# Transposing k and q of chunks 10 to 23 on VectorE, from blocked loads, in an attention and MLP kernel

## The chip, the cores and the metric

The kernel runs on one core of one Trainium2 chip. The metric is the device time of one execution in microseconds (us). Each version is run several times, and its median counts. The profile shows one further execution.

## What is computed

A linear attention with decay, followed by a two-layer MLP with a leaky ReLU, all in 32-bit floats:

```python
# q, k, v: (B, H, S, D) = (4, 8, 768, 64); lam: one decay per head; blocks of 64 tokens
for b in range(S // 64):
    qb, kb, vb = (block b of q, k, v)
    intra = einsum('bhic,bhjc->bhij', qb, kb) * Dmask        # lam ** (i - j) where i >= j, else 0
    intra = einsum('bhij,bhjd->bhid', intra, vb)
    inter = einsum('bhid,bhde->bhie', qb * lam_pow, kv_state)
    out[block b] = intra + inter
    kv_state = lam ** 64 * kv_state + einsum('bhsd,bhse->bhde', kb * rev_pow, vb)
x = out, tokens by (heads * D)                               # 3072 x 512
h = x @ w_in                                                 # 512 x 2048
out = maximum(0.01 * h, h) @ w_out                           # 2048 x 512
```

The weights come as 64-bit words, which the kernel converts itself.

## The kernel before, in words

**Chunks and rounds.** The 3072 tokens are cut into 24 chunks of 128 tokens (`NCH`), six to a batch entry. Four chunks make a group of 512 tokens (`GC`, `T`), so there are six groups. Chunks 0 to 3 run alone, chunk 4 is begun early, and from then on `round_of(c)` holds one chunk's attention, in a software pipeline: it loads k and q of chunk c + 2 (`load_kq`), computes chunk c's outputs (`outputs`), and in between chunk c + 1's scores and state update (`scores`). From round 8 on, the transposes of chunk c + 2 follow these on TensorE. Matrix products of the attention are 64x64 products on quadrants of TensorE (`quad`, L286).

**Transposes.** The scores need k and q with the head dimension on the partitions (`kTs`, `qTs`), and the loads bring tokens on the partitions (`kqv`). `transposes(c)` makes four TensorE transposes for k (into the upper part of `po`) and four for q (into `pt`), all on L331. ScalarE copies them to SBUF (L340, L341). Then GpSimd scales k in place by the decay (L345), which the state update reads, and the transposed q into `qsTs` (L349). `kqv`, `kTs`, `qTs` and `qsTs` have two buffers each, for even and odd chunks. VectorE multiplies the scores with the decay mask (L375) and updates the state (L382).

**Projections.** A chunk's result leaves `po` as three parts, `xh`, `xl`, `xm` (L430 on ScalarE, L431 and L433 on VectorE), which carry the 32-bit precision through three passes of the matrix product. `up(g, p)` multiplies a group with one of eight blocks of `w_in` (L561): two blocks of 512 columns, each with a scaling on ScalarE between the passes (L579) and the leaky ReLU into one of two `gs` buffers (L582), after which SP stores the buffer to the scratch tensor `G` (L585). `down` (L620) runs when all `up` steps are done, and reads `G` back.

**Weights.** `to_float32` turns 64-bit words into 32-bit floats: a load into one of three buffers `raw`, three passes on ScalarE (L497, L499, L501) and two on VectorE (L503, L504). The `w_in` blocks are converted in the first 90 us. The `w_out` blocks (`w_out`) are converted during groups 2 and 3, one for every two `up` steps, and stored to a scratch tensor `WO` (L538), from where they are read late.

**What sets the order.** Nothing is issued as it is written. Each operation is given to a planner (`Plan.add`) with its engine, an estimated duration in us, and the names of the buffers it reads and writes. `Plan.emit` simulates the engines with these estimates, always takes the operation that can start first (the smaller rank, the place in the list `seq`, breaks ties), and issues all in that order. Each engine then works strictly through its own order. All DMA loads and stores apart from `w_in`'s are issued on SP's queue, so a load that has to wait there holds up all that is behind it.

Of the kernel before, what the change touches and what calls it, by code (L numbers as in the profile page):

```python
# [31 lines left out]
def _bc(ap, idx, n):  # L32
    a = [list(x) for x in ap.ap]
    return bass.AP(ap.tensor, ap.offset, a[:idx] + [[0, n]] + a[idx:])


class Plan:
# [23 lines left out]
    def add(self, eng, us, fn, reads=(), writes=(), rank=0.0):  # L61

        n, deps = len(self.ops), set()
        for k in reads:
            w, r = self.last.setdefault(k, [None, []])
            if w is not None:
                deps.add(w)
            r.append(n)
        for k in writes:
            w, r = self.last.setdefault(k, [None, []])  # L70
            if w is not None:
                deps.add(w)
            deps.update(r)
            self.last[k] = [n, []]
        deps.discard(n)
        ways = {eng: us} if isinstance(eng, str) else dict(zip(eng, us))
        if self.chain is not None:
            self.chains[self.chain].append(n)
        self.ops.append((ways, fn, deps, (self.rank + rank, n), set(writes)))
# [81 lines left out]
def kernel(  # L161
# [10 lines left out]
    nc = tc.nc  # L172
    P = 128
    B, H, SEQ, D = q.shape
    C, C2 = P, P // 2
    NCB = SEQ // C
    HP = H // 2
    d_model, d_ff = moe_w_in.shape
    KO = d_model // P
    NP = d_ff // (2 * P)  # L180
    NCH = B * NCB
    GC = 4
    NG = NCH // GC
    T = GC * C
# [3 lines left out]
    QS = 0  # L188
    KM = 1
    NRAW = 3  # L190
    HALF = (slice(0, D), slice(D, 2 * D))
    assert D == 64 and KO == HP == 4 and SEQ % C == 0 and NCH % GC == 0 and d_model == T == 512 and NP % 4 == 0

    pool = ctx.enter_context(tc.tile_pool(name="sb", bufs=1))
    psum = ctx.enter_context(tc.tile_pool(name="ps", bufs=1, space=bass.MemoryType.PSUM))
# [3 lines left out]
    def sb(shape, name, dt=F32):  # L199
        return pool.tile(shape, dt, name=name, tag=name)  # L200

    def ps(shape, name):
        return psum.tile(shape, F32, name=name, tag=name)


    pt = ps([P, HP, C], "pt")
# [6 lines left out]
    X = [[sb([P, KO, T], f"x{x}{i}", F32R) for x in "hlm"] for i in range(2)]  # L213
    raw = [sb([P, 2 * d_model], f"raw{i}") for i in range(NRAW)]
    lows = [sb([P, d_model], f"low{i}", I32) for i in range(2)]
# [11 lines left out]
    def part(n):  # L227
        nonlocal used
        used += n
        assert used <= NA, used  # L230
        return att[:, used - n:used]

    ident = part(P)
    kqv = [[part(H * D).rearrange("p (h d) -> p h d", h=H) for _ in range(2)] for _ in range(3)]
    kTs, qTs, qsTs = ([part(HP * C).rearrange("p (y t) -> p y t", y=HP) for _ in range(2)] for _ in range(3))
    sc = part(2 * HP * C2).rearrange("p (x y t) -> p x y t", x=2, y=HP)
    state = [part(HP * D).rearrange("p (y d) -> p y d", y=HP) for _ in range(4)]
# [21 lines left out]
    add = plan.add  # L259
# [10 lines left out]
    def factors_q():  # L270
        for i in range(2):
            nc.vector.tensor_copy(lam_p[HALF[i]], lam_h[HALF[i], i::2])
        for hp in range(HP):
# [11 lines left out]
    def quad(dst, rows, lhsT, rhs, cols, start=False):  # L285
        nc.tensor.matmul(dst[HALF[cols]], lhsT=lhsT[HALF[rows]], rhs=rhs[HALF[rows]], start=start, stop=True,  # L286
                         skip_group_check=True)
# [11 lines left out]
    def of(c):  # L299
        return c // NCB, c % NCB, c % 2  # L300
# [3 lines left out]
    def load_kq(c):  # L304
        b, n, i = of(c)
        for src, x, nm in ((k, 0, "k"), (q, 1, "q")):
            y, dst = src[b, :, n * C:(n + 1) * C, :], kqv[x][i]

            def go(y=y, dst=dst):
                for z in range(2):  # L310
                    nc.sync.dma_start(out=dst[:, z * HP:(z + 1) * HP, :], in_=y[z::2].rearrange("h p d -> p h d"))  # L311
            add("DMA", 1.15, go, [], [f"{nm}{i}"])

    def load_v(c):
        b, n, i = of(c)
# [3 lines left out]
    def transposes(c):  # L319
        b, n, i = of(c)  # L320
        tk, tq = kqv[0][i], kqv[1][i]
        if c < GC:
            z, key = bank[KT].rearrange("p (y t) -> p y t", y=HP), KT
            at = [z[:, y, :] for y in range(HP)]
        else:
            z, key = po[:, :, upper, :], "po"
            at = [po[:, y // 2, HP + y % 2 * 2:HP + y % 2 * 2 + 2, :].rearrange("p a t -> p (a t)") for y in range(HP)]

        def go(src, at):
            for y in range(HP):  # L330
                nc.tensor.transpose(out=at[y], in_=src[:, 2 * y:2 * y + 2, :].rearrange("p a d -> p (a d)"), identity=ident)  # L331

        add("PE", 0.44, lambda: go(tk, at), [f"k{i}"], [key])
        add("PE", 0.44, lambda: go(tq, [pt[:, y, :] for y in range(HP)]), [f"q{i}"], ["pt"])

        def copies():
            kT = kTs[i]
            into = kT if c < GC else kT.rearrange("p (t a) x -> p t (a x)", t=2)
            src = z if c < GC else z.rearrange("p t a x -> p t (a x)")
            add("ACT", 0.6, lambda: nc.scalar.copy(into, src), [key], [f"kT{i}"])  # L340
            add("ACT", 0.6, lambda: nc.scalar.copy(qTs[i], pt), ["pt"], [f"qT{i}"])  # L341
            kr = tk.rearrange("p (y x) d -> p y x d", x=2)
            nr = slice(0, C2 if n == NCB - 1 else P)
            add(*((("DVE", "POOL"), (0.7, 1.1)) if c < KM else ("POOL", 1.1)),
                lambda e="POOL": ENG[e].tensor_tensor(kr[nr], kr[nr], _bc(pow_k, 3, D)[nr], op=ALU.mult), ["fk"], [f"k{i}"])  # L345
            m = slice(1 if n == 0 else 0, 2)
            o, x = (z.rearrange("p y (t i) -> p y t i", t=2)[:, :, m, :] for z in (qsTs[i], pt if c < QS else qTs[i]))
            eng, e, us, dep = ("DVE", nc.vector, 0.7, "pt") if c < QS else ("POOL", nc.gpsimd, 1.2, f"qT{i}")
            add(eng, us, lambda: e.tensor_tensor(o, x, _bc(pow_q, 2, 2)[:, :, m, :], op=ALU.mult), ["fq", dep], [f"qsT{i}"])  # L349

        return copies
# [121 lines left out]
    n_raw = 0  # L473

    def to_float32(kind, p, h, dst, key, after=()):

        nonlocal n_raw
        j, n_raw = n_raw % len(raw), n_raw + 1
        r, low, kl = raw[j], lows[n_raw % 2], f"low{n_raw % 2}"
        d = dst.bitcast(I32)  # L480

        def load():
            r64 = r.bitcast(I64)
            if kind == "wi":
                nc.scalar.dma_start(out=r64.rearrange("p (k f) -> p k f", k=2),
                                  in_=w_in_r[:, 2 * h:2 * h + 2, p * 2 * P:(p + 1) * 2 * P])
            else:
                nc.sync.dma_start(out=r64, in_=moe_w_out[(2 * p + h) * P:(2 * p + h + 1) * P, :])

        def words(i, dt):  # L490
            return r.bitcast(dt).rearrange("p (n two) -> p n two", two=2)[:, :, i]

        def addend(dt, i):
            return low.bitcast(dt).rearrange("p (n two) -> p n two", two=2)[:, :, i]

        add("DMA", 1.6, load, after, [f"raw{j}"])
        add("ACT", 0.67, lambda: nc.scalar.activation(out=dst, in_=words(1, F32), func=AF.Abs, scale=2.0 ** -110),  # L497
            [f"raw{j}"], [key])
        add("ACT", 0.78, lambda: nc.scalar.activation(out=addend(U16, 0), in_=words(0, U32), func=AF.Copy, bias=0.0, scale=2.0 ** -29),  # L499
            [f"raw{j}"], [kl])  # L500
        add("ACT", 0.77, lambda: nc.scalar.activation(out=addend(F16, 1), in_=words(1, F32), func=AF.Copy, bias=0.0, scale=2.0 ** -100),  # L501
            [f"raw{j}"], [kl])
        add("DVE", 0.42, lambda: nc.vector.tensor_scalar(d, d, 3, None, op0=ALU.logical_shift_left), [], [key])  # L503
        add("DVE", 1.0, lambda: nc.vector.tensor_tensor(d, d, low, op=ALU.add), [kl], [key])  # L504
# [159 lines left out]
    nxt, n_out = 3 * GC, 0  # L664
    steps = [(g, p) for g in range(2, NG) for p in range(NP)]
    for n, (g, p) in enumerate(steps):
        while nxt < (g + 1) * GC:
            seq.append(("r", nxt))
            nxt += 1
        seq.append(("up", g, p))  # L670
        if nxt < NCH and nxt // GC < g + 2 and n % 2 == 0:
            seq.append(("r", nxt))
            nxt += 1
        if n_out < NP and n % 2 == 1:
            seq.append(("wo", n_out, ["G%d%d" % steps[n - 1]]))
            n_out += 1
        if g == NG - 1:
            seq.append(("wp", p))
# [5 lines left out]
    for n, x in enumerate(seq):  # L684
# [9 lines left out]
        elif x[0] == "wp":  # L694
            if not freed:
                add("DVE", 0.0, lambda: None, [], ATT + [f"gr{j}" for j in range(NR)])
                add("ACT", 0.0, lambda: None, [], [f"raw{j}" for j in range(NRAW)] + ["t0", "t1"])
                freed = True
# [37 lines left out]
```

## Time and profile before

The median is 626.6 us of three runs (626.16 to 628.88). The profiled execution has a span of 623.6 us.

| What | Value |
|---|---|
| Transposes on TensorE, L331 | 192 (96 into pt, 80 into po, 16 into b), 0.273 us each at the median, overlapping |
| Copies of transposes on ScalarE, L340 and L341 | 24 + 24, about 0.59 us each |
| Loads of k, and of q, on SP | 48 + 48 of 128 KB, landing after 4.0 and 3.7 us at the median |
| Loads of v on SP | 24 of 256 KB, landing after 3.9 us |
| Stores of gs to G on SP | 52, landing after 2.9 us at the median |
| DMA packets | 103,706, of which 78,560 under 512 bytes |
| Read from and written to HBM | 65.02 MB and 35.65 MB |

Line numbers (L331) are those of the kernel before. PE is TensorE's matrix products and PEld its weight loads, DVE is VectorE, ACT is ScalarE, POOL is GpSimd, and SPq is SyncE's queue, which issues DMA. In the lists of instructions, a name such as `att<-in_q_dram` gives what is written and what is read; most small SBUF tensors are parts of the one tensor `att`. In a timeline, a row holds the start in us, the duration in us, the engine, the line, the operation, the names, and how many instructions of one kind were joined (x4).

### The profile page before, as it was taken

What the parts mean: (1) busy time and instruction counts of PE and PEld (TensorE: products, weight loads), DVE (VectorE), ACT (ScalarE), POOL (GpSimd) and SP (SyncE); (2) the same over time, 40 slices, a digit from 0 to 9 for tenths busy, and PEclk for the clock granted to TensorE, in tenths of its full rate; (3) what the DMA queues carried; (4) which work ended last, traced back from release to release, by engine and by line L of the source; (5) the groups of instructions that cost most, each with busy time, mean ns of one, the idle gap of its engine ahead of it and who ended that gap; (6) DMA issues with size and microseconds to landing.
All of it is one profiled execution on the core that took longest, in us unless ns stands there. A gap on an engine that the chain in (4) does not pass through costs nothing.

```text
span 623.6 us, 13157 instructions
## 1 busy us (share of the span) xinstructions
PE 613.9 (98%) x5578; PEld 513.5 (82%) x5578; DVE 297.9 (48%) x366; ACT 281.2 (45%) x461; POOL 91.7 (15%) x95
## 2 busy tenths in 40 slices
PE   8899999999999999999999999999999999999997
PEld 7688888898888888888788888888888888888885
DVE  4799882400344333333145763735545454535531
ACT  3688875443577766664444722312222222314111
POOL 4852513300332222222000000000000000000000
PEclk9999999999999999999999999999999999999999
DMA  9998844632787778842455762432524333333201
GB/s 201 250 259 259 243 156 136 155 111 91 206 248 253 245 238 259 247 163 87 169 202 189 247 203 72 153 117 82 188 67 135 136 106 131 128 109 118 85 0 67
DMA packets 103706, 101.51 MB, mean 163 GB/s; under 512 B 78560, under 2 KB 80608, under 8 KB 103648
## 3 DMA queue, kind: packets, MB, share of 16 engines
q1 hardware_dynamic: 99152, 92.29, 47.3%
q10 hardware_dynamic: 4496, 8.39, 4.3%
q8 instruction: 43, 0.70, 0.5%
q14 instruction: 15, 0.12, 0.1%
HBM read 65.02 MB, written 35.65 MB: 161 GB/s over the span
## 4 chain that ended last, share of the span: by engine, by line
PE 96%; DMA 2%; SPq 0%; POOL 0%; DVE 0%; ACT 0%; issue 0%; DVEq 0%
PE b L561 43%; PE b L620 17%; PE po L620 11%; PE psc L620 10%; PE po L286 4%; PE pt L620 3%; PE psc L286 3%; PE po L331 2%; PE pt L331 2%; DMA att<-in_q_dram 2%; PE b L253 1%; DMA att<-in_k_dram 1%; SPq L311 0%; PE b L331 0%; POOL att L345 0%
## 5 line engine op out<-in xcount | busy, mean ns | idle before, releaser
L602 ACT ACTIVATE xh<-att 128x1024 fp32r<-128x1024 f32 x48 | 50.9, 1061 | 147.3 <-PE po L620 141.3
L603 DVE SCALAR_TENSOR_TENSOR xl<-att,xh 128x1024 fp32r<-128x1024 f32 x48 | 58.7, 1223 | 99.4 <-ACT xh L602 99.4
L561 PE MATMUL b<-xh,wh 128*128 128x512 f32 (+3 forms) x416 | 105.5, 377 | 0.0
L561 PE MATMUL b<-xl,wl 128*128 128x512 f32 (+3 forms) x416 | 105.4, 376 | 0.0
L561 PE MATMUL b<-xm,wm 128*128 128x512 f32 (+3 forms) x416 | 104.9, 381 | 0.0
L561 PEld LDWEIGHTS b<-xl,wl 128*128 128x128 f32 x416 | 75.5, 188 | 14.7 <-DVE wl L515 0.2
L561 PEld LDWEIGHTS b<-xh,wh 128*128 128x128 f32 x416 | 75.3, 188 | 14.3
L561 PEld LDWEIGHTS b<-xm,wm 128*128 128x128 f32 x416 | 73.5, 188 | 13.2
L579 ACT ACTIVATE b<-b 128x512 f32<-128x512 f32 (+2 forms) x98 | 56.7, 579 | 57.1 <-PE b L561 56.3
L582 ACT ACTIVATE gs<-b 128x512 f32<-128x512 f32 (+2 forms) x98 | 57.8, 590 | 48.7 <-PE b L561 40.2
L375 DVE TENSOR_TENSOR att<-psc,att 128x512 f32<-128x512 f32 x24 | 16.5, 688 | 128.3 <-PE psc L286 128.2
L620 PE MATMUL b<-wl,xl 128*128 128x512 f32 x192 | 74.7, 389 | 0.0
L620 PE MATMUL b<-wh,xh 128*128 128x512 f32 x192 | 74.7, 389 | 0.0
L605 DVE SCALAR_TENSOR_TENSOR xm<-xl,xh 128x1024 fp32r<-128x1024 f32 x48 | 58.8, 1226 | 4.8
L345 POOL TENSOR_TENSOR att<-att 128x512 f32<-128x512 f32 (+1 forms) x24 | 27.6, 1149 | 141.1 <-PE po L331 133.5
L620 PEld LDWEIGHTS b<-wh,xh 128*128 128x128 f32 x192 | 36.1, 188 | 7.5
L620 PEld LDWEIGHTS b<-wl,xl 128*128 128x128 f32 x192 | 36.0, 188 | 7.5
L385 POOL TENSOR_TENSOR att<-att 128x256 f32<-128x256 f32 x40 | 35.6, 889 | 28.7 <-DVE att L382 23.4
L620 PE MATMUL po<-wm,xm 128*128 128x512 f32 (+1 forms) x100 | 37.2, 381 | 0.7 <-ACT raw L642 0.7
L620 PE MATMUL psc<-wh,xh 128*128 128x512 f32 x96 | 37.4, 389 | 0.0
L620 PE MATMUL po<-wl,xl 128*128 128x512 f32 x96 | 37.4, 389 | 0.0
L620 PE MATMUL b<-wm,xm 128*128 128x512 f32 x96 | 37.4, 389 | 0.0
(67 smaller groups left out, 817.1 us busy)
## 6 DMA issues: line engine op xcount, KB each, us to landing
att<-g SPq DMA_DIRECT2D x48, 512.0 KB, 3.2
g<-gs SPq DMA_DIRECT2D x45, 512.0 KB, 2.9
raw<-in_moe_w_in_dram ACTq DMA_DIRECT2D x16, 512.0 KB, 5.0
raw<-in_moe_w_out_dram SPq DMA_DIRECT2D x16, 512.0 KB, 4.3
att<-in_k_dram SPq DMA_DIRECT2D x48, 128.0 KB, 4.0
att<-in_q_dram SPq DMA_DIRECT2D x48, 128.0 KB, 3.7
att<-in_v_dram SPq DMA_DIRECT2D x24, 256.0 KB, 3.9
out_dram<-gs SPq DMA_DIRECT2D x23, 256.0 KB, 2.2
```

What stands on the lines that cost most here:

```text
L286: nc.tensor.matmul(dst[HALF[cols]], lhsT=lhsT[HALF[rows]], rhs=rhs[HALF[rows]], start=start, stop=True, skip_group_check=True)
L331: nc.tensor.transpose(out=at[y], in_=src[:, 2 * y:2 * y + 2, :].rearrange("p a d -> p (a d)"), identity=ident)
L345: lambda e="POOL": ENG[e].tensor_tensor(kr[nr], kr[nr], _bc(pow_k, 3, D)[nr], op=ALU.mult), ["fk"], [f"k{i}"])
L375: add("DVE", 0.69, lambda: nc.vector.tensor_tensor(sc, psc[:, :, lower, :], decay, op=ALU.mult), ["psc", "fk"], ["sc"])
L385: add("POOL", 0.7, lambda new=new, j=j: nc.gpsimd.tensor_tensor(state[(j + 1) % 4], new, _bc(lam_c, 2, D), op=ALU.mult), [f"st{j % 4}", "f ...
L561: nc.tensor.matmul(dst, lhsT=w[z][:, kk * 2 * P + f * P:kk * 2 * P + (f + 1) * P], rhs=x[z][:, kk, toks], start=start and kk == 0, stop=kk ...
L579: add("ACT", ns, lambda b=b: nc.scalar.activation(out=b, in_=b, func=AF.Copy, bias=0.0, scale=S + 1.0), [], [kb], rank=-1.5)
L582: add("ACT", ns, lambda b=b, r=r: nc.scalar.activation(out=r, in_=b, func=AF.Prelu, bias=0.0, scale=1.0 / WS, alpha=0.01), [kb], [f"gs{jg} ...
L602: add("ACT", 1.05, lambda: nc.scalar.activation(out=h, in_=graw[j], func=AF.Copy, bias=0.0, scale=NEAR), reads, wr("h"))
L603: add("DVE", 1.25, lambda: nc.vector.scalar_tensor_tensor(l, graw[j], 1.0, h.bitcast(F32), op0=ALU.mult, op1=ALU.subtract), reads + [f"rh{ ...
L605: add("DVE", 1.25, lambda: nc.vector.scalar_tensor_tensor(m, l.bitcast(F32), -S, h.bitcast(F32), op0=ALU.mult, op1=ALU.add), [f"rh{j}", f" ...
L620: nc.tensor.matmul(acc[tb][z // 2][:, cols], lhsT=ring[j][z][:, f * T + tb * P:f * T + (tb + 1) * P], rhs=W[pp][z][:, f * d_model:(f + 1) ...
```

## The change

From chunk 10 on (`DV`), TensorE no longer transposes. VectorE transposes instead[...]. For the result to be a whole transpose, the blocks themselves have to lie in transposed order when VectorE reads them, and the DMA loads bring this about. For each pair of chunks k and q are loaded into a buffer `subs[0]` or `subs[1]` by 16 loads each: for every pair of heads `y` and every quarter `a` of the partitions, 32 partitions get 8 blocks of 32 floats (128 bytes) each. One VectorE instruction of 128x512 elements then makes `kTs` of a chunk, and one makes `qTs`, in SBUF; the ScalarE copies are gone.

- k is still loaded as before too, since GpSimd and the state update need it with tokens on the partitions. q isn't.
- `subs[1]` takes the place of the two q buffers. `subs[0]` takes the place of the third `raw` buffer, so that the conversion of `w_out` has two `raw` buffers in place of three.
- Each `subs` buffer holds two chunks and is single: a pair's loads wait until both chunks of the pair before have been transposed.
- The planner counts 4.0 us of DMA for 16 loads and 0.7 us of VectorE for a transpose.
- `w_out` blocks are converted one for every three `up` steps, in place of every two.

```diff
+    DV = 10
+    C4 = P // 4
...
-    kqv = [[part(H * D).rearrange("p (h d) -> p h d", h=H) for _ in range(2)] for _ in range(3)]
+    kqv_f = [part(2 * H * D) for _ in range(3)]
+    kqv = [[x[:, i * H * D:(i + 1) * H * D].rearrange("p (h d) -> p h d", h=H) for i in range(2)] for x in kqv_f]
+
+    subs = [x.rearrange("p (y t) -> p y t", y=HP) for x in (raw[-1], kqv_f[1])]
...
-            add("DMA", 1.15, go, [], [f"{nm}{i}"])
+            if nm == "k" or c < DV:
+                add("DMA", 1.15, go, [], [f"{nm}{i}"])
+            if c >= DV and c % 2 == 0:
+                def go_sub(src=src, sub=subs[x]):
+                    for y in range(HP):
+                        for a in range(4):
+                            h = y // 2 + (2 * y + a // 2) % HP * 2
+                            z = src[b, h, n * C:(n + 2) * C, a % 2 * C4:(a % 2 + 1) * C4]
+                            nc.sync.dma_start(out=sub[a * C4:(a + 1) * C4, y, :].rearrange("j (m i) -> j m i", i=C4),
+                                              in_=z.rearrange("(m j) i -> j m i", j=C4))
+                add("DMA", 4.0, go_sub, [], ["q0", "q1"] if nm == "q" else [f"raw{NRAW - 1}"])
...
-        add("PE", 0.44, lambda: go(tk, at), [f"k{i}"], [key])
-        add("PE", 0.44, lambda: go(tq, [pt[:, y, :] for y in range(HP)]), [f"q{i}"], ["pt"])
+        if c < DV:
+            add("PE", 0.44, lambda: go(tk, at), [f"k{i}"], [key])
+            add("PE", 0.44, lambda: go(tq, [pt[:, y, :] for y in range(HP)]), [f"q{i}"], ["pt"])
...
-            add("ACT", 0.6, lambda: nc.scalar.copy(into, src), [key], [f"kT{i}"])
-            add("ACT", 0.6, lambda: nc.scalar.copy(qTs[i], pt), ["pt"], [f"qT{i}"])
+            if c < DV:
+                add("ACT", 0.6, lambda: nc.scalar.copy(into, src), [key], [f"kT{i}"])
+                add("ACT", 0.6, lambda: nc.scalar.copy(qTs[i], pt), ["pt"], [f"qT{i}"])
+            else:
+                for sub, dst, ks, kd in ((subs[0], kTs[i], [f"raw{NRAW - 1}"], f"kT{i}"), (subs[1], qTs[i], ["q0", "q1"], f"qT{i}")):
+                    add("DVE", 0.7, lambda a=dst, b=sub: nc.vector.transpose(out=a, in_=b[:, :, i * C:(i + 1) * C]), ks, [kd])
...
-        j, n_raw = n_raw % len(raw), n_raw + 1
+        j, n_raw = n_raw % (len(raw) - (kind == "wo")), n_raw + 1
...
-        if n_out < NP and n % 2 == 1:
+        if n_out < NP and n % 3 == 1:
```

More of the change, by code (lines that the diff above doesn't have):

```diff
@@ L190 @@
     NRAW = 3
+    DV = 10
+    C4 = P // 4
     HALF = (slice(0, D), slice(D, 2 * D))
-    assert D == 64 and KO == HP == 4 and SEQ % C == 0 and NCH % GC == 0 and d_model == T == 512 and NP % 4 == 0
+    assert DV % 2 == NCB % 2 == 0 and D == 64 and KO == HP == 4 and SEQ % C == 0 and NCH % GC == 0 and d_model == T == 512 and NP % 4 == 0
     pool = ctx.enter_context(tc.tile_pool(name="sb", bufs=1))
```

## The prediction

> **What bounds the kernel now.** I read the page's busy lines first, then the chain of waits, then the timeline of the stage in which the change works.
>
> ```profile
> PE 613.9 (98%) x5578; PEld 513.5 (82%) x5578; DVE 297.9 (48%) x366; ACT 281.2 (45%) x461; POOL 91.7 (15%) x95
> ...
> PE 96%; DMA 2%; SPq 0%; POOL 0%; DVE 0%; ACT 0%; issue 0%; DVEq 0%
> ```
>
> TensorE (PE) is busy for 98% of the span and makes 96% of the chain that ended last. So what is taken off PE comes off the time, until something else makes PE wait. The next answer is PE's timeline, for a round of the attention with transposes and then for round 22, which has none any more:
>
> ```profile
> 195.17 0.93 PE L286 MATMUL po<-att 64*64 64x64 f32 x48
> ...
> 196.85 0.41 PE L286 MATMUL po<-att 64*64 64x64 f32 x16
> 197.19 0.66 PE L331 MATMUL po<-att 128*128 128x128 f32 x4
> 197.68 0.60 PE L331 MATMUL pt<-att 128*128 128x128 f32 x4
> 198.04 1.18 PE L561 MATMUL b<-xm,wm 128*128 128x512 f32 x4
> ...
> 292.89 0.93 PE L286 MATMUL po<-att 64*64 64x64 f32 x48
> ...
> 294.90 1.20 PE L561 MATMUL b<-xm,wm 128*128 128x512 f32 x4
> ```
>
> Eight transposes hold PE from 197.19 to 198.04: 0.85 us. Their durations overlap, so the start-to-start time is what counts. Rounds 12 to 21 start 13.97 us apart (195.17 less 181.19); round 22 lasts from 292.89 to 306.01, 13.12 us. The same two projection steps lie in each. Both readings give 0.85 us per round. Last, the same stage by stretches: a round with the down weights' conversion, one after it, and round 22 (columns: PE, PEld, DVE, ACT, POOL busy, clock, DMA share, GB/s):
>
> ```profile
> 195.17:209.14 13.97, 13.97 (x186) 11.71 (x185) 5.63 (x9) 10.01 (x18) 3.98 (x4) 1.00 0.78 247
> 278.91:292.89 13.98, 13.98 (x186) 11.72 (x185) 3.69 (x5) 6.34 (x12) 3.51 (x4) 1.00 0.28 96
> 292.89:306.01 13.12, 13.12 (x161) 10.88 (x160) 2.31 (x4) 5.48 (x10) 0.00 (x0) 1.00 0.27 92
> ```
>
> VectorE (DVE) has half its time free. The DMA engines, at 0.78, do not.
>
> [...] The trace of before has no 128-byte packet.
>
> **Part 1, transposes leave PE.** Chunks 10 to 23 are transposed in rounds 8 to 21: 14 rounds by 0.85 us = 11.9 us, all on the path. The two ScalarE (ACT) copies of 0.59 us (L340, L341) go too, which ends nothing, since ACT is busy 10.0 of 13.97 us. POOL's scaling of k (L345) loses its wait for PE.
>
> **Part 2, VectorE.** Each chunk gains two transposes of 128x512 elements. The nearest row is L375, 128x512 f32 in 0.688 us; the upper end is two passes, 1.4 us. I take 0.69. Per pair of chunks 4 x 0.69 = 2.8 us are added to 2 x 5.6 us, in 26.2 us: it is hidden. The conversion takes some away again, as below. They are queued on VectorE in the planner's order. A transpose waiting for its load holds up xl, xm (L431, L433) and the conversion (L503, L504); PE wants those only in the next round, some 10 us later.
>
> **Part 3, DMA engines.** The trace's packet records give medians of 9 ns at 32 bytes, 18 ns at 256, 27 ns at 512 and 159 ns at 4096. The line through 32 and 256 gives 13 ns at 128 bytes; the ends are 9 ns and[...] 18 ns. Per pair of chunks two q loads of 1,024 packets go (2,048 x 18 ns / 16 engines = 2.3 us of all engines) and 32 blocked loads of 256 packets come (8,192 x 13 / 16 = 6.7 us; 4.6 to 9.2). k is now loaded twice, since its token layout is still needed. The conversion goes from one block per two steps to one per three: a block is 3 x 128 packets of 4096 bytes, 3 x 128 x 159 / 16 = 3.8 us, so 2.0 blocks per pair of rounds become 1.33, less 2.5 us. Before: 0.78 x 27.95 = 21.8 us. After: 21.8 - 2.3 + 6.7 - 2.5 = 23.7 of 26.2 us, a share of 0.90, between 0.82 and 1.00. This is close, but beneath PE.
>
> **Part 4, the SP queue.** All these loads are issued by SP, in one order, and this is where PE could be made to wait.
>
> ```profile
> 195.92 0.38 SPq L316 DMA_DIRECT2D att<-in_v_dram  x1
> 196.42 1.73 SPq L311 DMA_DIRECT2D att<-in_k_dram  x2
> 198.25 1.44 SPq L311 DMA_DIRECT2D att<-in_q_dram  x2
> 199.93 0.34 SPq L585 DMA_DIRECT2D g<-gs  x1
> ...
> 206.30 0.32 SPq L585 DMA_DIRECT2D g<-gs  x1
> ```
>
> An issue takes at least 0.37 us for k and q (the answer for L311: 367/508/1707) and some 0.05 us lie between two. So 16 blocked loads take 16 x 0.42 = 6.7 us where the planner counts 4.0, and 32 take 13.4 us. The records also show eight semaphores in turn: each load waits on SP for the one eight earlier to have landed. A k or q load lands in 3.9 us at the median (2.3 to 6.9); at 3.9 eight per landing are 0.49 us each, 15.6 us for 32; at 4.8 it is 0.60 and 19.2 us. The rest of SP's work in a pair is, from the durations above, about 7 us. Together 20 to 23 of 26 us.
>
> Who is queued behind? The stores of gs (L585). The activation that rewrites a gs buffer (L582) waits for its store, and behind it on ACT stands the scaling (L579) that PE needs. The blocked loads become free when the odd chunk's transposes have run, about 4.3 us after a round's start. A store leaves before them at 3.9 us (199.93 less 195.17, less 0.85). The next is due at 10.3 us (206.30 less 195.17, less 0.85). Its buffer is rewritten 12.4 us later in the trace (218.73), 11.6 without the transposes; less 2.9 us to land, it bears 8.7 us of delay. With 0.42 us per load both groups are out at 4.3 + 13.4 = 17.7 us: 7.4 us late, no stall. With 0.49: 9.9 us of 20 less 10.3, 1 us too late, and PE has about that much slack. With 0.60: 13.2 us late, 4.5 us too many. The blocked buffers themselves have time: filled from about 4 us, wanted three rounds after the round in which they became free.
>
> **The early rounds.** raw2 is last read by the up weights' conversion near 88 us, and chunk 10's blocks are wanted by round 9 at 104.4. That is 16 us for 6.7 of issue and a landing. Hidden, with one or two microseconds in doubt.
>
> **Cases.**
> - A, PE keeps the gain: 626.6 - 11.9, plus about 1 us for landings that come late here and there: 615.5. Chance 0.60. For it: slack in every sum above.
> - B, bursts on SP hold up the gs stores by 1 us too much in each of six pairs, or the first blocks come late: 614.7 + 6 = 620.7. Chance 0.15. For it: the planner's 4.0 us where I count 6.7. Against it: a store due within a group goes ahead of the next group, by its rank.
> - C, transfers become the bound. At 18 ns a packet the DMA share is 1.00, landings lengthen, 0.60 us per load and a stall of 3 to 4.5 us in each of six pairs: 614.7 + 18 = 632.7, up to 641. Slower. Chance 0.17.[...]
> - D, VectorE: its queue, blocked some 4 us per pair because a transpose stands before its late q blocks, delays po's readers, 1.5 us reach PE: 614.7 + 6 x 1.5 = 623.7. About the same as before. Chance 0.08.
>
> **The numbers.** The time is A's, 615.5. Everything removed and nothing lost would be 614.7; 614.0 allows for the scatter (626.16 to 628.88 before). The top must take in B and D and the start of C: 628. Faster by over 0.5% (below 623.5): A, B and part of D, 0.77. Within: 0.07. Slower (above 629.7): most of C, 0.16.
>
> **What would show it.** L331 on PE falls from 192 to 80 transposes; rounds 12 to 21 are 13.1 us apart; 28 transposes appear on VectorE at about 0.69 us; 43,008 more packets; PE without gaps from 160 to 300 us. If PE waits there for ACT, and ACT for the store of gs, B or C holds; if PE waits for att from VectorE's transposes or for po's readers, D. A DMA share near 1.00 with landings above 4.8 us is C. The prediction is wrong if an issue on SP takes much over 0.5 us in the groups, or if a 128-byte packet takes 18 ns or more.

## The result, and the profile after

The changed kernel takes 657.9 us at the median (656.2 to 659.2), the kernel before 626.4 us in the same comparison (626.2 to 628.9). The ratio is 1.049, with a 95% interval of 1.045 to 1.053. The change makes the kernel about 31 us slower, where the prediction was 615.5 us.

The page of the changed kernel, its busy lines and its chain of waits:

```profile
PE 614.2 (94%) x5466; PEld 509.7 (78%) x5466; DVE 314.1 (48%) x399; ACT 265.3 (41%) x428; POOL 90.1 (14%) x95
...
DMA packets 149851, 105.20 MB, mean 161 GB/s; under 512 B 124704, under 2 KB 126752, under 8 KB 149792
...
PE 80%; SPq 9%; DMA 7%; issue 2%; ACT 1%; DVE 1%; POOL 0%; DVEq 0%; ACTq 0%
PE b L582 32%; PE b L641 17%; PE po L641 10%; PE psc L641 10%; SPq L326 8%; PE pt L641 3%; PE po L292 3%; PE psc L292 3%; DMA g<-gs 3%; DMA att<-in_q_dram 2%; DMA raw<-in_moe_w_out_dram 1%; DMA att<-in_v_dram 1%; PE pt L347 1%; PE b L259 1%; DMA att<-in_k_dram 0%
```

TensorE (PE) fell from 96% to 80% of the chain. In its place SP's queue appears with 9%, nearly all of it on one line, L326, which issues the blocked loads, and DMA rose from 2% to 7%. Where nothing disturbs a round, the change does what it was made for. In PE's timeline of such a round the projections (L582) follow the attention's products (L292) at once, and rounds start 13.14 us apart (198.37 less 185.23):

```profile
185.23 0.93 PE L292 MATMUL po<-att 64*64 64x64 f32 x48
...
186.91 0.41 PE L292 MATMUL po<-att 64*64 64x64 f32 x16
187.26 0.97 PE L582 MATMUL b<-xm,wm 128*128 128x512 f32 x3
...
198.37 0.93 PE L292 MATMUL po<-att 64*64 64x64 f32 x48
```

The loss is elsewhere. Between 60 and 345 us (columns as before: length, busy times of PE, PEld, DVE, ACT and POOL, clock, DMA share, GB/s) the changed kernel has:

```profile
60.00:345.00 285.00, 255.03 (x3125) 212.95 (x3124) 110.32 (x176) 135.13 (x244) 59.32 (x62) 0.94 0.66 179
```

PE is idle for 30 us of this stretch, where before it had 284.72 us of work in it, and its granted clock is 0.94. The DMA engines are busy to 0.66, so they are not full.

Where the idle time comes from is seen in its longest piece, 10.16 us in round 10. PE's timeline, then the waits of PE's own sequencer (PEldq, from the answer for L292: shortest, median and longest in ns), then SP's timeline and ScalarE's (ACT):

```profile
112.44 0.93 PE L292 MATMUL po<-att 64*64 64x64 f32 x48
123.53 1.87 PE L292 MATMUL psc<-att 64*64 64x64 f32 x46 [10.16 <-issue]
```

```profile
L292 PEldq EVENT_SEMAPHORE  x25: 51/51/10534, 6.9 to 323.4; - x25
```

```profile
99.75 0.46 SPq L606 DMA_DIRECT2D g<-gs  x1
100.35 9.05 SPq L326 DMA_DIRECT2D raw<-in_k_dram  x16
109.50 9.23 SPq L326 DMA_DIRECT2D att<-in_q_dram  x16
118.83 0.39 SPq L606 DMA_DIRECT2D g<-gs  x1
119.32 0.39 SPq L332 DMA_DIRECT2D att<-in_v_dram  x1
119.82 1.71 SPq L317 DMA_DIRECT2D att<-in_k_dram  x2
```

```profile
99.87 1.10 ACT L603 ACTIVATE gs<-b 128x512 f32<-128x512 f32 x2 [1.69 <-DMA g<-gs]
...
122.28 0.38 ACT L603 ACTIVATE gs<-b 128x256 f32<-128x256 f32 x1 [13.08 <-DMA g<-gs]
122.56 0.59 ACT L600 ACTIVATE b<-b 128x512 f32<-128x512 f32 x1
123.07 0.17 ACT L435 COPY att<-po 128x2 f32<-128x2 f32 x1
```

SP was issuing 32 blocked loads from 100.35 to 118.73, and all else stood behind them. The longest wait of PE's sequencer, 10.534 us, is this gap. In the trace it ends at 123.47 and is for a load's semaphore; the load of v that SP issued at 119.32 landed at 123.44. So it was v that PE waited for.

A store was as late. The gs buffer that ACT had filled by 100.97 us was to be stored at once. The store left at 118.83, and the next activation into that buffer (L603) waited 13.08 us. Behind it in ACT's order stood the tiny copy L435, for which PE waits in a round. It ended at 123.24, 0.2 us before v came: had v been there, PE would have stood still almost as long, for a store that none of its work needs.

In the same way the semaphores in the trace tell what ended the other gaps. Of PE's 30.4 us of gaps between 30 and 600 us, two that end with a load of v make 15.3 us. Five end with an activation (L600 or L603) behind a late store of gs, 7.1 us. Two end with the copy L435, 7.4 us: there it stood on VectorE behind the conversion of the down weights (L524), whose load was late as well. The list of waits shows what was late over the whole kernel:

```profile
POOL att L366 <- DMA att<-in_k_dram: 57.5, 9, 15.6
...
DVE att L362 <- DMA att<-in_q_dram: 43.3, 6, 11.3
ACT gs L603 <- DMA g<-gs: 41.1, 11, 13.1
```

Stores of gs, token-ordered loads of k, and the blocked q were all waited for. In the kernel before, the list has no wait of ACT for a store of gs, and one of GpSimd (POOL) for k, of 0.8 us.

Last, what one blocked load costs on SP, and one transpose on VectorE (DVE), from the answers for L326 and L362:

```profile
L326 SPq DMA_DIRECT2D att<-in_q_dram x112: 312/449/2272, 75.7 to 298.4; - x112
L326 SPq DMA_DIRECT2D raw<-in_k_dram x112: 311/449/1711, 87.4 to 280.2; - x112
...
DMA to landing us min/median/max: 1.6/2.0/6.6
```

```profile
L362 DVE STREAM_TRANSPOSE att<-att x14: 662/700/712, 88.2 to 302.0; 128x512 f32<-128x512 f32 x14
L362 DVE STREAM_TRANSPOSE att<-raw x14: 669/706/712, 99.0 to 296.8; 128x512 f32<-128x512 f32 x14
```

**The sum.** The profiled spans are 654.4 and 623.6 us. With the 11.9 us that PE gave up, 42.7 us have to be explained. PE's idle gaps between 30 and 600 us add up to 30.4 us (0.3 before). In the four longest gaps the clock records fall to half, once for 13.65 us and three times for 6.83. PE worked for 20.5 us in that state, in which the 128x512 products of a projection start 0.427 us apart at the median, for 0.227 at full clock: by this estimate nearly half of it, some 10 us, is lost. Together that is about 40 of the 42.7 us.

### The profile page after: what moved, and what is told of

Read it like the earlier page. It is cut to its first block, busy times and chain, and to the rows that moved or that the text cites. A ratio compares the mean times of both kernels' runs of the same rounds, so it can differ in the third digit from the quotient of the medians.

```text
span 654.4 us, 13163 instructions
## 1 busy us (share of the span) xinstructions
PE 614.2 (94%) x5466; PEld 509.7 (78%) x5466; DVE 314.1 (48%) x399; ACT 265.3 (41%) x428; POOL 90.1 (14%) x95
## 3 DMA queue, kind: packets, MB, share of 16 engines
q1 hardware_dynamic: 145296, 95.97, 50.5%
## 4 chain that ended last, share of the span: by engine, by line
PE 80%; SPq 9%; DMA 7%; issue 2%; ACT 1%; DVE 1%; POOL 0%; DVEq 0%; ACTq 0%
PE b L582 32%; PE b L641 17%; PE po L641 10%; PE psc L641 10%; SPq L326 8%; PE pt L641 3%; PE po L292 3%; PE psc L292 3%; DMA g<-gs 3%; DMA att<-in_q_dram 2%; DMA raw<-in_moe_w_out_dram 1%; DMA att<-in_v_dram 1%; PE pt L347 1%; PE b L259 1%; DMA att<-in_k_dram 0%
## 5 line engine op out<-in xcount | busy, mean ns | idle before, releaser
L582 PE MATMUL b<-xh,wh 128*128 128x512 f32 (+3 forms) x416 | 108.9, 386 | 5.6 <-ACT gs L603 5.6
L582 PE MATMUL b<-xm,wm 128*128 128x512 f32 (+3 forms) x416 | 106.4, 387 | 1.9 <-ACT b L600 1.9
L582 PE MATMUL b<-xl,wl 128*128 128x512 f32 (+3 forms) x416 | 108.0, 383 | 0.0
L582 PEld LDWEIGHTS b<-xh,wh 128*128 128x128 f32 x416 | 77.0, 194 | 21.5 <-ACT gs L603 6.6
L603 ACT ACTIVATE gs<-b 128x512 f32<-128x512 f32 (+2 forms) x98 | 56.9, 587 | 86.3 <-PE b L582 44.0
L582 PEld LDWEIGHTS b<-xl,wl 128*128 128x128 f32 x416 | 77.6, 193 | 15.4 <-DVE wl L536 0.2
L582 PEld LDWEIGHTS b<-xm,wm 128*128 128x128 f32 x416 | 74.4, 191 | 17.7 <-ACT b L600 3.1
L600 ACT ACTIVATE b<-b 128x512 f32<-128x512 f32 (+2 forms) x98 | 55.8, 577 | 58.3 <-PE b L582 58.0
L292 PE MATMUL psc<-att 64*64 64x64 f32 x1472 | 30.1, 229 | 16.5 <-issue 10.2
L370 POOL TENSOR_TENSOR att<-att 128x512 f32<-128x512 f32 (+1 forms) x24 | 29.6, 1232 | 109.4 <-PE po L292 95.0
L292 PE MATMUL po<-att 64*64 64x64 f32 x1472 | 33.8, 225 | 8.1 <-DVE att L435 7.7
L292 PEld LDWEIGHTS psc<-att 64*64 64x64 f32 x1472 | 27.5, 143 | 17.8 <-issue 16.0
L292 PEld LDWEIGHTS po<-att 64*64 64x64 f32 x1472 | 27.9, 136 | 16.2 <-DVE att L435 8.3
L366 POOL TENSOR_TENSOR att<-att 128x512 f32<-128x512 f32 (+1 forms) x24 | 27.7, 1154 | 81.4 <-DMA att<-in_k_dram 57.5
```

What stands on the lines that cost most here:

```text
L582: nc.tensor.matmul(dst, lhsT=w[z][:, kk * 2 * P + f * P:kk * 2 * P + (f + 1) * P], rhs=x[z][:, kk, toks], start=start and kk == 0, stop=kk ...
L600: add("ACT", ns, lambda b=b: nc.scalar.activation(out=b, in_=b, func=AF.Copy, bias=0.0, scale=S + 1.0), [], [kb], rank=-1.5)
L603: add("ACT", ns, lambda b=b, r=r: nc.scalar.activation(out=r, in_=b, func=AF.Prelu, bias=0.0, scale=1.0 / WS, alpha=0.01), [kb], [f"gs{jg} ...
```

## The experiments

Theory SP: a blocked load costs SP 0.45 us and a gap of 0.05, for its issue and not for what it moves. A group of 16 is issued in one run, and stores and loads of other work stand behind it. Rivals: the 128-byte packets fill the DMA engines; VectorE's transposes, or their place in its order, hold up PE; SP is too small for all issues, however they are ordered; the planner's new order by itself. All runs below are timed against the kernel before; the lines are shown with their surroundings left out.

### One load in place of 16

```diff
-                    for y in range(HP):
-                        for a in range(4):
...
-                            nc.sync.dma_start(out=sub[a * C4:(a + 1) * C4, y, :].rearrange("j (m i) -> j m i", i=C4),
-                                              in_=z.rearrange("(m j) i -> j m i", j=C4))
+                    z = src[b].rearrange("h s d -> (h s) d")[n * C * 8:(n * C + 2 * C) * 8]
+                    nc.sync.dma_start(out=sub.rearrange("p y t -> p (y t)"), in_=z.rearrange("(p m) d -> p (m d)", p=P))
```

> The changed kernel, but each group of 16 blocked loads is replaced by one load of 512 KB in rows of 4096 bytes (so k and q of chunks 10 to 23 hold other data than they should). VectorE's transposes and all waits on the data stay. Theory SP (the 16 issues of a group, 9 us in one run on SP's queue, hold up the stores and loads behind them): 614 to 618 us, no gap on PE above 1 us between 100 and 340 us. Rival packets (128-byte packets fill the DMA engines): the same 614 to 618, as the packets are gone too. Rival VectorE (the transposes themselves, or their place in VectorE's order, hold up PE): stays above 640.

Measured: 615.45 us (614.58 to 617.21), ratio 0.983 (0.981 to 0.985). PE's idle gaps between 30 and 600 us are 0.7 us. With transposes, waits and the conversion all in their places, the predicted gain is there in full. VectorE's transposes as the cause fall. So does the planner's order by itself, since the plan is that of the changed kernel, operation for operation. Packets and issues are both gone here, so these two are left.

### The same packets from a quarter of the issues

```diff
-                    for y in range(HP):
-                        for a in range(4):
...
+                    for y in range(HP):
+                        z = src[b, 2 * y:2 * y + 2, :, 0:C4].rearrange("h s d -> (h s) d")[0:8 * P]
+                        nc.sync.dma_start(out=sub[:, y, :].rearrange("p (m i) -> p m i", i=C4),
+                                          in_=z.rearrange("(m p) i -> p m i", p=P))
```

> The changed kernel, but each group of 16 loads of 256 packets is made as 4 loads of 1,024 packets of 128 bytes over 128 partitions (the bytes and packets of the group are the same, their places are not, so the data are not k and q as they should be). Theory SP: a group takes about 4 x 0.5 = 2 to 4 us of SP, the time is 615 to 620. Rival packets: no change from 657, or not under 645. This run tells the two apart.

Measured: 615.48 us (614.54 to 616.12), ratio 0.983 (0.981 to 0.984). The stretch from 60 to 345 us, two shorter ones in it, and two groups on SP:

```profile
60.00:345.00 285.00, 283.28 (x3299) 237.71 (x3298) 135.41 (x202) 158.93 (x283) 59.26 (x62) 1.00 0.75 210
180.00:206.00 26.00, 24.94 (x331) 20.39 (x329) 9.29 (x17) 13.30 (x24) 5.75 (x7) 1.00 0.94 243
206.00:232.00 26.00, 26.00 (x342) 21.51 (x335) 11.56 (x20) 15.39 (x27) 5.51 (x6) 1.00 0.88 234
```

```profile
209.64 2.64 SPq L324 DMA_DIRECT2D raw<-in_k_dram  x4
...
217.91 3.36 SPq L324 DMA_DIRECT2D att<-in_q_dram  x4
```

As many packets of 128 bytes are moved, at a higher DMA share (0.75 against 0.66), and PE is busy for 283.28 of 285 us. The packets are not the cause. The plan is again that of the changed kernel. The 14 groups take SP 3.7 us at the mean (2.5 to 7.6), where those of 16 loads took 9.4. The places in memory differ too, so this run alone does not settle it; the run further below that only adds issues does.

### The loads of a group planned singly

```diff
+    SUB_US = 0.5
...
+                ks = ["q0", "q1"] if nm == "q" else [f"raw{NRAW - 1}"]
+                add("POOL", 0.0, lambda: None, [], ks)
+                for y in range(HP):
+                    for a in range(4):
+                        def go_sub(y=y, a=a, src=src, sub=subs[x]):
...
-                add("DMA", 4.0, go_sub, [], ["q0", "q1"] if nm == "q" else [f"raw{NRAW - 1}"])
+                        add("DMA", SUB_US, go_sub, ks[:1], [f"part{x}{y}{a}"])
```

> The changed kernel with the same 16 loads per group, but each is an operation of its own in the plan, at 0.5 us, so that stores and other loads may go between them on SP's queue; the plan now counts 8.0 us per group. Theory SP: the stores leave in time, PE's waits fall to under a third of the 31 us, 620 to 632 us. Rival packets, or SP too small for all its issues however they are ordered: above 645.

Measured: 633.2 us (631.9 to 636.0), ratio 1.012 (1.009 to 1.014). The idle gaps fall from 30.4 to 12.0 us, somewhat more than the third that was expected to be left, and the time is 1 us above the expected range. The order of the same issues alone is worth 24.6 us. What is left is in part the same thing again. In one of the two longest gaps, 4.35 us from 252.55 us, PE waits for v, and SP's timeline shows the v load behind 16 loads that came to stand in a row after all:

```profile
245.04 7.84 SPq L329 DMA_DIRECT2D att<-in_q_dram  x16
252.98 1.35 SPq L335 DMA_DIRECT2D att<-in_v_dram  x1
```

### The stores of gs on ScalarE's queue

```diff
-            lambda: nc.sync.dma_start(out=G[g][p].rearrange("p (f t) -> p f t", f=2)[:, :, toks], in_=y), ...
+            lambda: nc.scalar.dma_start(out=G[g][p].rearrange("p (f t) -> p f t", f=2)[:, :, toks], in_=y), ...
```

> The changed kernel, with one word changed: the stores of gs are issued by ScalarE's queue in place of SP's. Theory SP: the gs buffers are no longer held (ScalarE waited 41 us for them in 11 waits), but v, k and w_out loads still stand behind the groups: 625 to 642. Rival VectorE or packets: no better than 652, since the stores' place then does not matter.

Measured: 648.7 us (647.2 to 651.8), ratio 1.035 (1.033 to 1.037): better than the change by 9 us, less than expected. ACT's waits for gs stores fall from 41.1 us to 2.9. But the longest gap of PE stays as it was, and here the timeline names v. PE's waits for v in the list, and one of SP's own waits:

```profile
115.00 0.93 PE L292 MATMUL po<-att 64*64 64x64 f32 x48
126.19 1.12 PE L292 MATMUL psc<-att 64*64 64x64 f32 x18 [10.27 <-DMA att<-in_v_dram]
```

```profile
PE psc L292 <- DMA att<-in_v_dram: 14.7, 2, 10.3
```

```profile
SPq L326 <- DMA g<-gs: 16.6, 8, 2.8
```

The loads of v still stood behind the groups and ended 14.7 of the 27.5 us of gaps that are left. And the move had a cost of its own. In the trace of the changed kernel the 490 loads and stores that SP and ACT issue share eight semaphores. Of the 482 that take one up again, 458 do so at the eighth issue (264 of 286 in the kernel before), and all are issued after the transfer that had it before has landed. With the stores on ACT, SP now waited 16.6 us, in eight waits, for stores that ACT had issued. How much of the time that is was not measured.

### Issues only, in the kernel before

```diff
             add("DMA", 1.15, go, [], [f"{nm}{i}"])
+            if c >= 10 and c % 2 == 0:
+                def go_more(src=src, x=x):
+                    for y in range(HP):
+                        for a in range(4):
+                            nc.sync.dma_start(out=spare[a * 32:(a + 1) * 32, x, y, :], in_=src[b, 2 * y, n * C:n * C + 32, 0:32])
+                add("DMA", 4.0, go_more, [f"{nm}T1"], [f"more{x}"])
```

> The kernel before, with everything it does, plus two groups of 16 small loads (32 packets of 128 bytes each, into a spare tile that nobody reads) for every pair of chunks from chunk 10 on, planned at 4.0 us a group like those of the change. No transposes move, nothing waits for these loads. Theory SP (the count of issues in one run costs, whoever uses the data): each issue takes 0.33 to 0.5 us, a group 6 to 8 us, and the time rises to between 632 and 665. Rivals (the cost comes from the packets, from waits on the blocked data, or from VectorE): 626 to 629.

Measured: 677.1 us (673.9 to 677.8), ratio 1.080 (1.077 to 1.083). Loads of 4 KB that nobody reads cost the kernel before 50 us, more than the upper end expected. From the answer for their line, the list of waits, and ACT's and SP's timelines of one gap (5.79 us of PE, from 154.56 us):

```profile
L318 SPq DMA_DIRECT2D spare<-in_q_dram x112: 311/419/2497, 75.7 to 323.3; - x112
L318 SPq DMA_DIRECT2D spare<-in_k_dram x112: 310/420/1754, 86.7 to 314.0; - x112
```

```profile
ACT gs L589 <- DMA g<-gs: 43.6, 12, 7.8
```

```profile
149.22 7.56 SPq L318 DMA_DIRECT2D spare<-in_q_dram  x16
156.88 1.18 SPq L592 DMA_DIRECT2D g<-gs  x2
```

```profile
159.71 0.60 ACT L589 ACTIVATE gs<-b 128x512 f32<-128x512 f32 x1 [7.76 <-DMA g<-gs]
```

An issue of 32 packets takes 0.42 us, one of 256 packets 0.45 us: the cost is that of an issue, hardly of what it moves. No transpose was moved, no data was waited for, the extra packets are 7,168 in place of 57,344, and ACT waits for gs stores as long as in the changed kernel. This shows the cause without the change. (The added operations also shift the planner's order here; in the runs with one and with four loads a group the plan was kept, and the loss was gone.) Not explained is why these issues cost 8 us more than those of the change.

### q alone, its group whole and its loads planned singly

The first run is the changed kernel without k's blocked loads; the second also has the loads of the group planned one by one, as above.

```diff
-            if c >= DV and c % 2 == 0:
+            if nm == "q" and c >= DV and c % 2 == 0:
...
+        add("PE", 0.44, lambda: go(tk, at), [f"k{i}"], [key])
         if c < DV:
-            add("PE", 0.44, lambda: go(tk, at), [f"k{i}"], [key])
             add("PE", 0.44, lambda: go(tq, [pt[:, y, :] for y in range(HP)]), [f"q{i}"], ["pt"])
```

> Only q of chunks 10 to 23 comes by blocked loads and VectorE; k stays on TensorE, with its third raw buffer back for the conversion. One group of 16 issues per pair in place of two, in one run, at the plan's 4.0 us. Half the transposes leave PE: 14 x about 0.4 = 5.6 us, so 620.6 without stalls. Theory SP, with the tolerance of 8.7 us worked out for a store: a run of 9 us that starts at 4.3 us ends at 13.3, 3 us late for the store due at 10.3, which is borne: 620 to 624. Rival (any group in one run stalls PE, whatever the tolerance): half of the 43 us lost stays, 638 to 645.

Measured: 627.1 us (624.7 to 628.5), ratio 1.000 (0.999 to 1.002). Neither case: 3 us above the first, 11 below the second. ACT still waits 10.6 us for stores, in six waits of at most 3.1 us, and the profiled execution has 3.9 us of idle gaps. A run of one group is nearly borne, and costs about what half of the transposes brings.

> The same with the 16 loads of a group planned singly, at 0.5 us each. Theory SP: 620 to 622, no worse than the run with the group whole; this is the version that may beat the kernel before. Rival: above 626.

Measured: 620.1 us (619.9 to 621.1), ratio 0.990 (0.989 to 0.992). With 16 issues per pair that let others in between, PE's gaps are 0.6 us and the gain of half the transposes is whole.

### The conversion of the down weights alone

```diff
-        j, n_raw = n_raw % len(raw), n_raw + 1
+        j, n_raw = n_raw % (len(raw) - (kind == "wo")), n_raw + 1
...
-        if n_out < NP and n % 2 == 1:
+        if n_out < NP and n % 3 == 1:
```

> The kernel before with only the conversion of the down weights changed: one block for every three steps, and two raw buffers for it. Every theory but one has this part cost nothing: 625.5 to 627. Rival (the later or slower conversion holds up what follows): above 628.

Measured: 626.1 us (625.6 to 627.9), ratio 1.000 (0.998 to 1.001). This part of the change costs nothing and brings nothing by itself.

### Three more orders of the queue

> The changed kernel with the 16 loads of a group planned singly (which alone gave 633.2), and the 16 loads of the down weights issued by ScalarE's queue in place of SP's. Theory SP: with these off the queue the rest of PE's waits shrinks further, 622 to 632. Rival (what is left in the split version are blocked loads that come too late for the scores, whatever else is on SP): 632 to 636.

```diff
-                nc.sync.dma_start(out=r64, in_=moe_w_out[(2 * p + h) * P:(2 * p + h + 1) * P, :])
+                nc.scalar.dma_start(out=r64, in_=moe_w_out[(2 * p + h) * P:(2 * p + h + 1) * P, :])
```

Measured: 641.7 us (639.9 to 644.1), ratio 1.024, worse than either reading. In its longest gap (8.56 us from 255.63 us) PE waits for a v load that again stands behind 16 q loads. A line of SP's own waits follows:

```profile
248.06 12.70 SPq L329 DMA_DIRECT2D att<-in_q_dram  x16
260.86 0.40 SPq L335 DMA_DIRECT2D att<-in_v_dram  x1
```

```profile
SPq L329 <- DMA raw<-in_moe_w_out_dram: 19.6, 5, 4.6
```

The 12.70 us are not all issuing. SP stood still from 252.45 to 256.54, before the tenth of the 16 loads. The semaphore whose turn it was had gone to a load of the down weights that ACT issued only at 252.96, and that landed at 256.52. There are five such waits of SP, 19.6 us in all, where the split version has one of 0.6. So the run made room on SP's queue and at once tied it to ACT's; it does not tell whether room was what the split version lacked.

> The changed kernel with the 16 loads of a group planned singly at 0.3 us in place of 0.5 (633.2 us), so that the plan's DMA is not overfull. If the rest of the loss in that version comes from the plan's own order: 622 to 630. If it comes from SP's real time for 32 issues per pair, which a lower estimate only hides: 633 to 645.

```diff
-    SUB_US = 0.5
+    SUB_US = 0.3
```

Measured: 646.0 us (644.5 to 648.2), ratio 1.032 (`SUB_US` is the estimate for one load in the split version). An estimate further below the real 0.5 us makes the order worse by 13 us, just past the second reading. Idle gaps rise from 12.0 to 19.1 us. So an overfull plan was not the trouble; that SP's real time for the issues is what is left fits, but is not shown by this run alone.

> The version with q alone, singly planned (620.1 us), from chunk 8 on in place of 10. Two more chunks leave PE by about 0.43 us each. Theory SP: 619 to 621 if the loads of chunks 8 and 9 find room near 65 us, where the DMA engines are 0.83 busy; rival: that stage has none, 621 to 626.

```diff
-    DV = 10
+    DV = 8
```

Measured: 624.4 us (622.7 to 628.7), ratio 0.997 (0.996 to 0.998), 4.3 us slower than the same from chunk 10 on. Its gaps (5.4 us in all, four of them between 36 and 91 us) lie in a stage where the DMA engines are full (0.90 between 75 and 90 us): the rival expectation.

### q from chunk 10 on, k from chunk 20 on

q by blocked loads from chunk 10 on, k only for chunks 20 to 23, all loads planned singly:

```diff
-            if c >= DV and c % 2 == 0:
+            if c >= (KV if nm == "k" else DV) and c % 2 == 0:
...
-        if c < DV:
+        if c < KV:
             add("PE", 0.44, lambda: go(tk, at), [f"k{i}"], [key])
+        if c < DV:
```

> q as in the version with its loads planned singly (620.1 us), and k by blocked loads too, singly planned, but only for chunks 20 to 23. Theory SP: two pairs get a second group, when the queue has least else to carry; 4 chunks x about 0.43 = 1.7 us more leave PE: 618 to 621. Rival: the second group of a pair always costs more than it brings: 622 to 626.

Measured: 617.95 us (617.8 to 619.5), ratio 0.987 (0.985 to 0.989), the fastest of the versions that compute the whole.

```profile
60.00:345.00 285.00, 284.72 (x3330) 240.14 (x3329) 125.06 (x185) 167.91 (x296) 59.08 (x62) 1.00 0.67 198
```

PE is busy for 284.72 of 285 us, as in the kernel before, with fewer transposes in it, and the clock is full.

## Why the prediction was wrong

**What bounds, and part 1, right.** 80 transposes are left on PE, and undisturbed rounds start 13.14 us apart, for 13.12 predicted. The two runs that took the issues away without giving PE anything back measured 615.45 and 615.48 us, where case A said 615.5. Packets rose by 46,145 and not by 43,008: the 196 additional loads bring 16 packets of 4 bytes each (7,568 of these on SP's queue, for 4,432 before), which that forecast left out.

**Part 2, VectorE, right in its durations.** 28 transposes of 128x512 at 0.70 us, for 0.69 taken: about as long as the plain 128x512 product L375 (0.69 us), from which the part had it. From the blocks of 32 by 32 that the loads had put in transposed order, one such instruction makes a chunk's whole `kTs` or `qTs`. What the part overlooked is the tiny copy (L414 before, L435 after). The planner gives it to VectorE or to ScalarE, and PE wants it in the same round, not in the next.

**Part 3, DMA engines, right.** The 57,344 packets of 128 bytes take 13 ns at the median, 11 to 13 at the ends (5% and 95%), whether their half row starts at byte 0 or at byte 128 of its row. In the run with four loads a group every half row starts where its row starts, and the packets of the queue take as long in all: 53.7% of 614.3 us, for 50.5% of 654.4. So the part's upper end of 18 ns, the median of a 256-byte packet, doesn't appear. (The part read 9 ns for 32 bytes; that is the median of the 4-byte packets, those of 32 bytes have 7, and its line would then give 12 ns.) In the same run, where PE isn't held up, the share was 0.94 and 0.88 in the two stretches of 26 us, for 0.90 predicted, and PE worked for 24.94 and 26.00 us of them: close, but beneath PE, as the part said. The mechanism of case C didn't occur: in the changed kernel the share was 0.66 between 60 and 345 us, and a blocked load lands in 2.0 us.

**Part 4, the SP queue, is the step that failed.** It named the right queue, one of the right victims (gs stores, L582 and L579 before, L603 and L600 after) and a right way to PE, and then found 7.4 us of delay bearable. Measured, the runs of loads cost 42.7 us. Four terms were wrong.
- An issue was taken as 0.42 us, from the smallest issue of k and q, in a line whose medians are 0.51 and 0.46. The median of a blocked load is 0.449, with 0.045 to the next: 0.49, which was one of the values worked out. On top, one to five issues of a group took over 0.5 us, up to 2.3. The 14 groups last 9.4 us at the mean (7.8 to 11.7), for 6.7: 0.59 per load. That is the 0.60 which the part worked out too, 4.5 us too many, and left to slow landings and case C. Its sum of SP's work, 20 to 23 of 26 us, leaves this value out; with it SP is full at 26. (In the sum for 0.49, 20 less 10.3 is 9.7, not 9.9.)
- The 8.7 us that a store can bear were read from the steady stage, for a store that is due 6 us after the groups start. In rounds 8 to 11 the `up` steps are cut into pieces of one to three chunks, and stores come at other times. The buffer filled by 100.97 us was wanted at 109.2, 8.2 us later, not 11.6, and its store came just behind the start of the groups at 100.35. It left 17.9 us late. That is where the longest gap lies.
- The stores were taken as the only victim behind the groups; the loads of v, k and the down weights were not followed. But v ended 15.3 us of PE's gaps, the longest among them, and the late down weights, by way of the tiny copy, 7.4; the stores ended 7.1. With the stores out of the way, PE still waited 10.27 us for v at the same place.
- The price of a gap was taken as the gap. In the trace of the changed kernel the clock fell to half in the four gaps of 3.43, 5.09, 6.67 and 10.16 us, and in none of the others, of 1.59 us at most; about 10 of the 42.7 us are this, by the estimate above. Over all runs here it fell with each of the 15 gaps of 3.2 us and more between 90 and 300 us. With shorter ones it was not always so: in the run that only adds issues one of 2.32 us came with a fall, and one of 3.09 us with none.

**The cases.** B had the right source, bursts on SP, with one of its victims, and 6 us in place of 43; C, the slower case, reached to 641 and for another reason. D's pattern, one of po's readers held up in VectorE's order, occurred in the two gaps of the tiny copy, but behind the conversion: no transpose ended a gap of over 0.3 us. The range followed B and not B's cause taken further: the spread of an issue's time, 0.42 to 0.60, was only carried through the steady stage and only for one victim.

**The remark on the planner** was nearer than the case made of it. The plan counted 4.0 us for 9.4, and kept 16 loads together. Planned singly, the same loads gave back 24.6 us.

What stays open: what freeing one victim alone would bring, since they hide one another, as v and the copy do within 0.2 us; and why single issues in a group take 1 to 2 us. The trace goes some way there. It isn't the turn of the semaphores: before each of the 15 issues of over 1 us the transfer that had the same semaphore before had landed. But 13 of the 15 fell together with a transfer of 16 KB on the instruction queue (`q8 instruction` in the page, 43 in all) and ended 0.4 to 0.7 us after it; of the 202 issues of under 0.65 us, 11 overlap one. How such a transfer holds up an issue isn't shown.

## What to carry to other kernels

A DMA issue has a price on the queue that makes it, here 0.5 us whether it moves 4 KB or 32 KB; before a load is split into many, multiply by their count and ask what stands behind the run in that queue, at every stage and not only in the steady one. Where a planner emits many issues as one operation, make them separate operations with their real price, so that urgent loads and stores can pass. Moving transfers to another queue isn't free either when both draw on the same semaphores in turn: the two runs that did so made SP wait 16.6 and 19.6 us for ACT's transfers. And when PE is the bound, count a gap of several microseconds at more than its length: here about 10 us of slow clock came on top of 30 us of gaps.

## What the runs showed that was not expected

- 224 extra issues of 4 KB each, read by nobody, slowed the kernel before by 50.6 us (677.1 against 626.5): 0.23 us per issue, on a queue that is not on the path when it flows.
- The price of an issue hardly depends on its packets up to some hundreds: 0.42 us at 32, 0.45 us at 256. At 1,024, in the run with four loads a group, the medians are 0.60 for k and 0.79 for q.
- For a blocked load the issue, 0.45 us, is more than twice the work on each DMA engine, 16 packets of 13 ns or 0.2 us (an estimate from 256 packets over 16 engines), though the 2.0 us from issue to landing are longer than either. For how many such loads the queue passed, the issue decided: a group of 16 took SP 9.4 us at the mean, and as many packets in four issues 3.7.
